# Set attention, then a SoLU layer: product sums of three groups in one PSUM bank, gathers riding with scores, rows scaled by two engines

## The chip, the cores and the metric

The kernel runs on one core of one Trainium2 chip. The metric is the device time of one execution, in microseconds (us); less is better. TensorE is called PE here, VectorE DVE, ScalarE ACT, GpSimd POOL, and SyncE, which issues the transfers, SP.

## The reference

Everything is float32. `x` is 4 x 12608 x 128, there are 32 inducing points, and the layer is 1024 wide.

```python
def mab(q, kv):                       # scale = 1 / sqrt(128)
    s = scale * (q @ kv.transpose(0, 2, 1))
    s = s - s.max(-1, keepdims=True)
    a = np.exp(s)
    a /= a.sum(-1, keepdims=True) + 1e-09
    return a @ kv
h = mab(I, x)                         # 32 inducing points attend to x: first attention
x = mab(x, h)                         # x attends to the 32 rows of h: second attention
h = x @ w_in                          # 128 -> 1024: first layer
e = np.exp(h - h_max)                 # h_max: maximum of the row
solu = h * (e / (e.sum(-1) + 1e-09))
ln = (solu - mean) / np.sqrt(var + 1e-06) * g_ln
out = ln @ w_out                      # 1024 -> 128
```

## The kernel before

Each batch has 12608 rows, which are 99 tiles of 128 (the last is half a tile). The kernel is a set of Python generators, one for each chain of work, and a `Planner` that runs them on a model of the engines before anything is issued: each `Op` names an engine, an assumed cost, what it waits for and a priority, and the planner picks, for the engine that is free first, the ready operation of the lowest priority number (ready within `SLACK` of that engine). The order in which it picks is the order in which the instructions stand on each engine's queue, and each queue runs in that order. Constants named `PR_...`, `SLACK`, `BEAT`, `SWITCH` and so on only steer this order. A `Lock` is a pool of buffers; taking one makes the next instruction wait for the last reader of it.

The work, by generator:

- `p1(b, k)`: first attention on a group of up to 16 tiles (12 in batch 0, which runs first and by itself, "early"). It loads x (`xn`), turns it on PE (L583 in row mode, L614 early), copies it (L593 on ACT), stores the transposed x to DRAM (`xd`, L624), computes the scores (L643), takes the maximum of each column block (L659), brings the four blocks' maxima together with a small product against the matrix `fold` (L663 on DVE, L668 on PE, L677 and L684 on DVE), takes the exp (L694), transposes it on DVE (L714), and sums x with these weights on PE (L725, "the gather"), which DVE adds to a running sum (L741). Groups of the next batch run between the tiles of this one.
- `combine(b)`: finishes h for a batch and folds it into w_in (L772 scales the sum, L790 is the product).
- `p2(b, j)`: second attention's weights for 16 tiles: loads the transposed x back (L818), scores (L833), maximum, subtraction on POOL (L845), exp (L852), turns (L875), copy to `aT` (L889).
- `main()`: for each tile the first layer (L1009), eight products on two of PE's four row blocks, into one of four PSUM buffers `h` of 128 x 1024.
- `soft(...)`: DVE scales the row and finds its extreme (L1050), ACT takes the exp (L1061), POOL multiplies (L1065), ACT squares and sums (L1076), DVE transposes 32 x 32 blocks into `vt` (L1089). A row's buffers come from the pools `HN` and `EU`.
- `products(b, j, t, w)`: four tiles are a group `j`; its second-layer products (L1132) are 4 x 32 of 32 rows against `wc`, with the row sum as a 129th column. The four row blocks `a` go in two pairs `w`, each pair into one `h` buffer. `beats` issues them in beats: in each beat one product of both row blocks of pair 0 and of pair 1, or of one pair while `also`, the first layer or a turn, uses the other pair's row blocks. A beat in which only two of the four row blocks work is called a half beat below.
- `evacuate(...)`: copies a group's pair (2 x 129 columns) from PSUM to `spare`, on DVE or ACT (L1155).
- `floor`: sends the groups' sums of squares through DRAM to their places (`dd`, `dl`).
- `finish(b, f)`: for five groups (`FG`) small ACT and POOL operations make the inverse deviation `y` (L1177 to L1191), then POOL scales each group's rows (L1198), and `stored` writes 256 KB.

PE's scores, gathers and fold products use other modes than the row mode of the rest; the planner adds `SWITCH` for each such visit.

Of the kernel before, what the change touches and what calls it, by code (L numbers as in the profile page):

```python
# [14 lines left out]
ALU = mybir.AluOpType  # L15
# [4 lines left out]
P = 128  # L20
# [14 lines left out]
SWITCH = 400  # L35

# [19 lines left out]
HN_MORE = 4  # L56
# [12 lines left out]
PR_G2 = 8  # L69
PR_HN = -4  # L70
PR_MU = -4
PR_SQ = 4
PR_TU = 12
# [8 lines left out]
WIN = -18.5  # L82
# [8 lines left out]
DMA_LAG = 1800  # L91
# [159 lines left out]
def set_attention_then_solu_kernel(ctx: ExitStack, tc: tile.TileContext, x, inducing, w_in, w_out, g_ln, out):  # L251
# [67 lines left out]
    EW = Lock()  # L319
    ST = Lock([  # L320
# [9 lines left out]
    SM = Lock([small(i, mloc=1, mdiag=4, junk=4, nb=1, fac=1, ls=1, rl=1) for i in range(4)])  # L330
# [200 lines left out]
    turned = [Event() for _ in range(NP[0])]  # L531

    def p1(b, k):
# [35 lines left out]
        def by_rows(ways):  # L569
# [4 lines left out]
            def turn():  # L574
                w = min(ways, key=lambda w: (load(w) > 0, w))
# [9 lines left out]
                beats(-(-n // 2), (1 - w,), two)  # L585

# [47 lines left out]
        if not early:  # L634
            (eT, ew), erel = yield lew
# [11 lines left out]
        d = yield Op("PE", (0 if early else SWITCH) + n * 60, scores, ready, rel, ind_ready.after)  # L647
# [9 lines left out]
        for lo, hi, nn in parts:  # L657
            d = yield Op(
                "DVE", 411, lambda: nc.vector.tensor_reduce(out=v["mloc"][lo:hi], in_=sc[lo:hi, : nn * M], op=ALU.max, axis=AX.X), dsc  # L659
            )  # L660
        d = yield Op(
            "DVE", 131,
            lambda: nc.vector.tensor_scalar(  # L663
                out=v["mdiag"], in0=quarter, scalar1=v["mloc"], scalar2=None, op0=ALU.mult, op1=ALU.max, accum_out=v["nb"]
            ),
            d,
        )
        d = yield Op("PE", (80 if early else SWITCH) + 110, lambda: nc.tensor.matmul(mq, lhsT=fold2, rhs=v["mdiag"], start=True, stop=True), d)  # L668
# [6 lines left out]
        d = yield Op(  # L675
            "DVE", 122,
            lambda: nc.vector.tensor_scalar(  # L677
                out=v["junk"], in0=mq, scalar1=(-3.0e38 if first else mold), scalar2=None, op0=ALU.max, op1=ALU.max, accum_out=mnew
            ),
            d, prev,  # L680
        )
        plan.set(chain[b][k + 1], d)
        dm = d = yield Op(
            "DVE", 70, lambda: nc.vector.tensor_scalar(out=v["nb"], in0=mnew, scalar1=-scale, scalar2=None, op0=ALU.mult), d  # L684
        )
        df = None
        if early:
            (eT, ew), erel = yield lew
# [9 lines left out]
        de = d = yield Op("ACT", (130 + 35 * n) * len(parts) + (0 if first else 190), exps, dm, erel)  # L698
# [15 lines left out]
        d = yield Op("DVE", 435, lambda: nc.vector.transpose(out=ew[:, :n, :].rearrange("p s m -> p (s m)"), in_=eT[:, : n * M]), d)  # L714
        nq = min(4, n)
        rel = None
        if not early:
            give(lpb, big, de)
            big, rel = yield lpb
        pooled = big[:, 512 - C : 512]  # L720

        def gather():
# [6 lines left out]
        dp = yield Op("PE", 74 * n, gather, d, rel)  # L729
# [20 lines left out]
        give(lpb, big, da)  # L750
# [9 lines left out]
    def combine(b):  # L760
# [11 lines left out]
        d = yield Op("DVE", 200, lambda: nc.vector.tensor_scalar(out=accn, in0=acc, scalar1=rl, scalar2=None, op0=ALU.mult), d, prev)  # L772
# [33 lines left out]
    def p2(b, j):  # L806
# [4 lines left out]
        for k, (g0, gn) in enumerate(p1_groups[b]):  # L811
# [47 lines left out]
        def turned_rows():  # L859
# [4 lines left out]
            def turn():  # L864
                w = min(ways, key=lambda w: (load(w) > 0, w))
# [11 lines left out]
                beats(-(-pairs // 2), (1 - w,), two)  # L877

# [40 lines left out]
    stream = [dict(j=JB, emit=None, ready=0.0, close=None) for _ in range(2)]  # L919
    flow = {"idle": Event(), "left": 2 * NB * NG, "prio": 0.0}  # L920

    def load(w):
        p = stream[w]
        return JB - p["j"] if p["j"] < JB and p["ready"] <= plan.now + EAGER else 0

    def beats(count, pairs=(0, 1), also=None):

        for i in range(count):
            if also:
                also(i)  # L930
            went = False
            for w in pairs:
                p = stream[w]
                if p["j"] < JB and p["ready"] <= plan.now + i * BEAT + EAGER:
# [381 lines left out]
```

## Time and profile before

| | us |
|---|---|
| median of 3 runs | 1245.16 (1244.42 to 1248.59) |
| the profiled execution | 1244.09 |
| its span in the profile | 1242.3 |
| busy PE / DVE / ACT / POOL | 1196.1 / 1092.8 / 1085.6 / 1087.8 |
| busy share PE / DVE / ACT / POOL | 96% / 88% / 87% / 88% |
| granted PE clock | 0.979 |
| DMA moved | 113.61 MB, mean 91 GB/s |

Busy time counts every stretch in which at least one instruction of the engine runs. Matmuls overlap each other and their ends are modelled, so PE's share says little about how much of its peak is used. In a view of instruction groups a row reads: line, engine, operation, output and input by the program's names, shape, count, busy time and mean ns of one, and idle time in front of it with what ended it. A wait "A <- B: 28.2, 29, 6.1" means that A's engine stood 28.2 us in all, 29 times and at most 6.1 us, until B was done.

### The profile page before, as it was taken

The page shows a single profiled execution, that of the slowest core. Times are in us where ns is not written, and L with a number is a line of the kernel's source. Part 1 is how long each engine was busy: PE and PEld are TensorE (multiplying, and loading weights), DVE is VectorE, ACT ScalarE, POOL GpSimd, SP SyncE. Part 2 cuts the span into 40 slices and gives each one's busy share as a digit, 9 for nine tenths or more (in the row PEclk, how much of TensorE's full clock was granted, in tenths as well). Part 3 has the DMA queues.
Part 4 walks back from the last instruction along what each step waited for, and adds up shares of the span by engine and source line. Part 5 has one row for each costly group of instructions (what it writes and reads, how often), then busy time and mean ns, then how long its engine had stood idle before and what let it go on. Part 6 is the DMA issues. An engine that isn't in the chain of part 4 may idle for free. (4 is left out here: it accounts for less than half of the span.)

```text
span 1242.3 us, 77962 instructions
## 1 busy us (share of the span) xinstructions
PE 1196.1 (96%) x35557; PEld 1112.9 (90%) x35557; DVE 1092.8 (88%) x1684; ACT 1085.6 (87%) x2152; POOL 1087.8 (88%) x638
## 2 busy tenths in 40 slices
PE   9999999999999989999999999999999999999995
PEld 7679999999998988998999899999899999999995
DVE  5689999999897989899988889989899999898982
ACT  5489998999897979898889889999888999998983
POOL 3478898988987878989898898989898999998996
PEclk9969999999999999999999999999999999989998
DMA  9663243321234233331223333523220212112013
GB/s 355 234 166 111 72 135 90 101 68 38 81 90 130 82 102 110 94 104 50 73 56 108 103 112 101 158 57 110 63 54 16 73 48 61 47 19 48 6 47 85
DMA packets 152908, 113.61 MB, mean 91 GB/s; under 512 B 76257, under 2 KB 132609, under 8 KB 148097
## 3 DMA queue, kind: packets, MB, share of 16 engines
q1 hardware_dynamic: 152576, 108.62, 29.2%
q8 instruction: 278, 4.55, 1.6%
q14 instruction: 54, 0.43, 0.1%
HBM read 54.30 MB, written 52.18 MB: 86 GB/s over the span
## 5 line engine op out<-in xcount | busy, mean ns | idle before, releaser
L1132 PE MATMUL h<-wc,vt 32*128 32x129 f32 (+1 forms) x25600 | 1030.4, 275 | 22.4 <-issue 13.7
L1132 PEld LDWEIGHTS h<-wc,vt 32*128 32x128 f32 (+1 forms) x25600 | 992.7, 186 | 60.6 <-issue 38.6
L1065 POOL TENSOR_TENSOR eu<-spare,eu 128x1024 f32<-128x1024 f32 x227 | 535.7, 2376 | 45.3 <-ACT eu L1061 45.0
L1089 DVE STREAM_TRANSPOSE vt<-eu 128x1024 f32<-128x1024 f32 x396 | 481.6, 1230 | 13.5 <-POOL eu L1065 12.9
L1076 ACT ACTIVATE sq<-eu 128x1024 bf16<-128x1024 f32 x396 | 416.7, 1052 | 47.5 <-POOL eu L1065 37.0
L1009 PE MATMUL h<-hs,aT 32*128 32x128 f32 x6336 | 435.2, 276 | 4.1 <-ACT aT L889 1.7
L1065 POOL TENSOR_TENSOR eu<-hn,eu 128x1024 f32<-128x1024 f32 x169 | 399.7, 2377 | 38.9 <-ACT eu L1061 38.7
L1009 PEld LDWEIGHTS h<-hs,aT 32*128 32x128 f32 x6336 | 392.2, 189 | 23.2 <-issue 6.7
L1050 DVE TENSOR_SCALAR_CACHE_REDUCE spare<-h,rn 128x1024 f32<-128x1024 f32 x227 | 285.8, 1265 | 40.4 <-PE h L1009 23.8
L1061 ACT ACTIVATE eu<-spare,nm 128x1024 f32<-128x1024 f32 x227 | 259.1, 1142 | 10.3 <-DVE spare L1050 7.8
L1050 DVE TENSOR_SCALAR_CACHE_REDUCE hn<-h,rn 128x1024 f32<-128x1024 f32 x169 | 212.8, 1264 | 29.9 <-PE h L1009 17.0
L1061 ACT ACTIVATE eu<-hn,nm 128x1024 f32<-128x1024 f32 x169 | 192.9, 1142 | 7.4 <-DVE hn L1050 4.8
L1198 POOL TENSOR_TENSOR spare<-spare,fin 128x512 f32<-128x512 f32 x100 | 101.2, 1044 | 1.4
L1076 ACT ACTIVATION_READ_ACCUMULATOR sq<-eu 128x1 f32 x396 | 74.8, 189 | 0.0
L1155 ACT COPY spare<-h 128x258 f32<-128x258 f32 (+1 forms) x127 | 45.7, 364 | 29.4 <-PE h L1132 28.2
L583 PE MATMUL h<-ident,xn 32*128 32x32 f32 x1188 | 54.1, 225 | 0.3 <-issue 0.3
L583 PEld LDWEIGHTS h<-ident,xn 32*128 32x128 f32 x1188 | 50.4, 136 | 0.7 <-issue 0.5
L593 ACT COPY xT<-h 128x1024 f32<-128x1024 f32 (+2 forms) x42 | 37.8, 901 | 10.1 <-PE h L583 9.8
L1155 DVE COPY spare<-h 128x258 f32<-128x258 f32 (+1 forms) x73 | 30.2, 416 | 18.4 <-PE h L1132 18.0
L1061 ACT ACTIVATION_READ_ACCUMULATOR eu<-spare,nm 128x1 f32 x227 | 43.0, 190 | 0.0
L875 PE MATMUL h<-ident,a 32*128 32x32 f32 (+1 forms) x800 | 34.2, 221 | 1.4 <-ACT a L852 1.1
L889 ACT COPY aT<-h 128x512 f32<-128x512 f32 (+3 forms) x66 | 30.2, 472 | 5.6 <-PE h L875 5.5
(154 smaller groups left out, 655.2 us busy)
## 6 DMA issues: line engine op xcount, KB each, us to landing
out_dram<-spare SPq DMA_DIRECT2D x96, 256.0 KB, 3.7
xT<-xd SPq DMA_DIRECT2D x19, 1024.0 KB, 5.7
xn<-in_x_dram SPq DMA_DIRECT2D x15, 1024.0 KB, 6.3
xd<-xT SPq DMA_DIRECT2D x15, 1024.0 KB, 5.1
dl<-dd SPq DMA_DIRECT2D x396, 1.0 KB, 2.8
xd<-vt SPq DMA_DIRECT2D x7, 768.0 KB, 10.3
spare<-in_x_dram SPq DMA_DIRECT2D x5, 768.0 KB, 12.8
xT<-xd SPq DMA_DIRECT2D x5, 768.0 KB, 5.6
```

The source lines that it names most:

```text
L583: nc.tensor.transpose(out=tr[:, k * 512 + s * M : k * 512 + (s + 1) * M], in_=xn[r, s, :], identity=ident[r, r])
L593: lambda: nc.scalar.copy(xT.rearrange("c s (q t) -> c q s t", q=4)[:, 2 * w : 2 * w + 2, :n, :], tr.rearrange("c (k x) -> c k x", k=2)[:, ...
L875: nc.tensor.transpose(out=tr[:h, k * 512 + q * M : k * 512 + (q + 1) * M], in_=both, identity=ident[r, r])
L1009: nc.tensor.matmul(hp[:, cols], lhsT=aT[rows, i // 2, :], rhs=hs[rows, cols], start=True, stop=True)
L1050: lambda: nc.vector.tensor_scalar(out=hn, in0=hp, scalar1=rn, scalar2=None, op0=ALU.mult, op1=ALU.min, accum_out=nm),
L1061: "ACT", 1133, lambda: nc.scalar.activation(e, hn, AF.Exp, bias=nm, scale=-1.0, accum_out=G["qe"][:, s, 1:2]), d, rel, srel,
L1065: d = yield Op("POOL", 2330, lambda: nc.gpsimd.tensor_tensor(out=e, in0=hn, in1=e, op=ALU.mult), de, prio=t + PR_MU)
L1076: "ACT", 1040, lambda: nc.scalar.activation(sq, e, AF.Square, scale=1.0 / 32.0, accum_out=G["qe"][:, s, 0:1]), d,
L1089: lambda: nc.vector.transpose(out=G["vtb"][:, : n * FF].rearrange("p (j s t) -> p j s t", j=M, s=n)[:, :, s, :], in_=e.rearrange("p (a f) ...
L1132: nc.tensor.matmul(op[:rows, a - 2 * w, : C + 1], lhsT=vt[q, k, :], rhs=wc[q, k, :], start=(k == 0), stop=(k == JB - 1))
L1155: return lambda: eng(F["raw"][:rows, i0 : i0 + 2, :], op[:rows, :, : C + 1])
L1198: return lambda: eng.tensor_tensor(out=raw, in0=raw, in1=y[:, i0 : i0 + 4].unsqueeze(2).to_broadcast([rows, 4, C]), op=ALU.mult)
```

## The change

- *Products.* Up to three groups in a row (`SLOTS`; 3 and 2 of a finish's five, and 3, 1, 1 in a batch's last) share one `h` buffer per pair, at column offsets of 129. It is taken at the first group and copied once, after the last, by `evacuate` for all of them. `stream[w]` becomes a list, so that the next group's products follow without a gap where they are ready.
- *First attention after batch 0.* The four blocks' maxima are brought together by DVE with one-column reduces (L710 and the like, on 32 partitions) instead of `fold`; ACT scales the maximum. The gather of group k-1 is issued right behind the scores of group k, into the unused half of the same buffer; only a batch's last gather still has a visit of its own.
- *Transfers.* x, the transposed x and its reload go in pieces of four tiles, 256 KB (`PIECE`), at most four under way (`TOKENS`, `BULK`). Batch 0's are left as they were.
- *Scaling.* Scaling the rows has an alternative on ACT, four instructions of 128 columns (`each_quarter`); the planner takes the one that it expects to end first.
- Numbers: priorities, slacks, assumed costs, one `HN` buffer handed to `EU`, three first-layer turns (`MINE`) instead of two, only the nearest tile considered (`WINDOW_TILES`). `accn` is scaled by ACT.

The numbers move almost every row, so the order is shown at three places. On PE, in the first attention of batch 3, which runs between batch 2's tiles, the three visits before: scores (L643), fold (L668) and gather (L725), each between products (L1132) or first layer (L1009); `h_694` and so on are the four buffers.

```order
L1132 MATMUL h_694<-wc,vt 128x129 x4
L643 MATMUL h_697<-xT,indT 32x512 x4
L1009 MATMUL h_696<-hs_117,aT_94 128x128 x2
...
L1132 MATMUL h_695<-wc,vt 128x129 x2
L668 MATMUL h_697<-small_123,fold 128x4
L1132 MATMUL h_694<-wc,vt 128x129 x2
...
L1132 MATMUL h_696<-wc,vt 128x129 x2
L725 MATMUL h_697<-xn_68,ew 32x128 x16
L1009 MATMUL h_695<-hs_117,aT_94 128x128 x2
```

and in the changed program, where L668 is now the scores, L784 the gather, L1244 the products and L1115 the first layer:

```order
L1244 MATMUL h_652<-wc,vt 128x129 x2
L1244 MATMUL h_651<-wc,vt 128x129 x2
L668 MATMUL h_650<-xT,indT 32x512 x4
L784 MATMUL h_650<-xn_68,ew 32x128 x16
L1115 MATMUL h_649<-hs_117,aT_94 128x128 x2
L1244 MATMUL h_652<-wc,vt 128x129 x2
```

The gather of the group before stands directly behind the scores and in their buffer, and the fold row is gone. Over the whole order there are 21 fold rows fewer and 18 gathers without a visit of their own. The products, first layer and turns make 3974 beats with all four row blocks and 536 half beats before, 4063 and 358 after; half beats followed by a full one are 179 and 95.

On ACT, around a finish of five groups, before (L1061 exp, L1076 square, L1155 evacuation, L1177 to L1190 the inverse):

```order
L1076 ACTIVATE sq,qe_100<-eu 128x1024
L1180 ACTIVATE fin_111<-fin_111 128x20
L1155 COPY spare<-h_696 128x258
L1184 ACTIVATE fin_111<-fin_111 128x20
L1185 ACTIVATE fin_111<-fin_111 128x20
L1186 ACTIVATE fin_111<-fin_111 128x20
L1190 ACTIVATE fin_111<-fin_111 128x20
L1061 ACTIVATE eu,qe_102<-hn_82,nm_112 128x1024
```

and after (L1168 exp, L1183 square, L1322 scaling of two groups, L1272 evacuation):

```order
L1168 ACTIVATE eu,qe_106<-hn_81,nm_115 128x1024
L1183 ACTIVATE sq,qe_106<-eu 128x1024
L1322 ACTIVATE spare<-spare,fin_111 128x128 x8
L1168 ACTIVATE eu,qe_100<-hn_80,nm_112 128x1024
...
L1168 ACTIVATE eu,qe_100<-spare,nm_115 128x1024
L1272 COPY spare<-h_652 128x2x2x129
L608 COPY xT<-h_650 128x2x7x32
```

Eight instructions in a row scale two groups; the copy takes two groups at once. Of the 100 scalings 39 stand on ACT, of the evacuations 57 on ACT and 31 on DVE (127 and 73 before).

On SP, around a reload of the transposed x, before (L818 reload, L624 store, L364 load of x, L1106 and L1114 the sums of squares):

```order
L1106 DMA dd_105<-qe_104 128x8
L818 DMA xT_86<-xd 128x2048
L1114 DMA dl_110<-dd_105 32x4x2 x4
L1106 DMA dd_107<-qe_106 128x8
L1114 DMA dl_110<-dd_107 32x4x2 x4
L364 DMA xn_67<-in_x_dram 128x4x512
```

and after (L899, L642, L371, L1213, L1221):

```order
L642 DMA xd<-xT 128x512 x4
L1213 DMA dd_103<-qe_102 128x8
L1221 DMA dl_108<-dd_103 32x4x2 x4
L371 DMA xn_68<-in_x_dram 128x512 x3
L899 DMA xT_86<-xd 128x512
L1213 DMA dd_105<-qe_104 128x8
L371 DMA xn_68<-in_x_dram 128x512
L899 DMA xT_86<-xd 128x512 x2
```

Pieces of two transfers now alternate with each other and with the small ones; SP issues 912 transfers instead of 736.

The diff, cut to its core:

```diff
+OS_ACT = 1
+SLOTS = 3
+PIECE = 4
+TOKENS = 4
-HN_MORE = 4
+HN_MORE = 3
-PR_G2 = 8
+PR_G2 = 4
...
-SLACK = {"PE": 0, "ACT": 200, "DVE": 100, "POOL": 100, "SP": 0}
+SLACK = {"PE": 0, "ACT": 400, "DVE": 200, "POOL": 100, "SP": 0}
-WINDOW_TILES = 3
-MINE = 2
-OP_FIRST = -30
+WINDOW_TILES = 1
+MINE = 3
+OP_FIRST = -100
...
+        if not early:
+            halves = [(c, min(c + PIECE, n)) for c in range(0, n, PIECE)]
         for c0, c1 in halves:
             for nbytes, fn in move(b, s0 + c0, c1 - c0, xn[:, c0:, :], False):
-                d = yield dma(nbytes, fn, rel)
+                trel = () if early else (yield BULK)[1]
+                d = yield dma(nbytes, fn, rel, trel)
+                if not early:
+                    give(BULK, None, d)
...
+        def visit():
+            scores()
+            if before:
+                gathers[(b, k - 1)](big[:, 512 + P : 512 + P + C])
...
+            def near():
+                for g in range(1, 4):
+                    same(v["quart"][quad[0], g : g + 1], v["quart"][quad[g], 0:1])
...
+            def spread():
+                for g in range(1, 4):
+                    same(mnew[quad[g]], mnew[quad[0]])
...
     def products(b, j, t, w):
-        bank, rel = yield H.at(OP_FIRST + t)
-        op = bank.rearrange("p (k x) -> p k x", k=2)
+        slot, last = slot_of[j]
+        if slot == 0:
+            held[w] = yield H.at(OP_FIRST + t)
+            held[w] += ([],)
+        bank, rel, mine = held[w]
+        mine.append(j)
+        op = bank.rearrange("p (k x) -> p k x", k=2)[:, :, slot * (C + 1) : (slot + 1) * (C + 1)]
...
         def close(d):
-            spawn(evacuate(b, j, w, op, bank, d, t + PR_EV), t + PR_EV)
+            if last:
+                spawn(evacuate(b, mine, w, bank, d, t + PR_EV), t + PR_EV)
+                give(PAIR[w], None)
...
-        stream[w].update(j=0, emit=emit, ready=ready, close=close, prio=t + PR_G2)
+        stream[w].append(dict(j=0, emit=emit, ready=ready, close=close, prio=t + PR_G2))
...
+            def each_quarter():
+                for a in range(4):
+                    act(raw[:, a, :], raw[:, a, :], AF.Copy, scale=y[:, i0 + a : i0 + a + 1])
+
-            done = yield Op("POOL", 1000, scaled(nc.gpsimd), dy, prio=OS_PRIO)
+            done = yield Op("POOL", 1000, scaled(nc.gpsimd), dy, prio=OS_PRIO, alt=Op("ACT", 1010, each_quarter, dy, prio=OS_PRIO) if OS_ACT else None)
```

More of the change, by code (lines that the diff above doesn't have):

```diff
@@ L633, in p1 @@
             yield ind_ready
-        if not early:
-            (eT, ew), erel = yield lew
+        before = None
+        if not early and k:
+            before = yield weighed[(b, k - 1)]
         big, rel = yield lpb
@@ L645, in scores @@
                 )
-        d = yield Op("PE", (0 if early else SWITCH) + n * 60, scores, ready, rel, ind_ready.after)
+        def visit():
+            scores()
+            if before:
+                gathers[(b, k - 1)](big[:, 512 + P : 512 + P + C])
+        d = yield Op(
+            "PE", (SWITCH + 74 * (p1_groups[b][k - 1][1] if before else 0) if not early else 0) + n * 60, visit, ready, rel, ind_ready.after, before
+        )
+        if before:
+            pooled_in[(b, k - 1)] = big[:, 512 + P : 512 + P + C]
+            plan.set(gathered[(b, k - 1)], d)
         def free_xT():
@@ L727, in gather @@
                 )
-        dp = yield Op("PE", 74 * n, gather, d, rel)
+        if not early:
+            if k:
+                give(lpb, big, de, *p1_added[(b, k - 1)].after)
+            else:
+                give(lpb, big, de)
+        if early or k == NP[b] - 1:
+            rel = None
+            if not early:
+                big, rel = yield lpb
+            pooled = big[:, 512 - C : 512]
+            dp = yield Op("PE", (0 if early else SWITCH) + 74 * n, lambda: gather(pooled), d, rel)
+            own = True
+        else:
+            gathers[(b, k)] = gather
+            plan.set(weighed[(b, k)], d)
+            got = yield gathered[(b, k)]
+            dp, pooled, own = got[0], pooled_in[(b, k)], False
         give(lx, xn, dp)
@@ L749, in p1 @@
         da = yield Op("DVE", 263, add, dp, de, p1_done[b][k - 1].after if k else None)
-        give(lpb, big, da)
+        if own:
+            give(lpb, big, da)
+        plan.set(p1_added[(b, k)], da)
         dl = yield l_done[b][k]
@@ L771, in combine @@
         prev = yield p1_done[b][NP[b] - 1]
-        d = yield Op("DVE", 200, lambda: nc.vector.tensor_scalar(out=accn, in0=acc, scalar1=rl, scalar2=None, op0=ALU.mult), d, prev)
+        d = yield Op("ACT", 200, lambda: nc.scalar.activation(accn, acc, AF.Copy, scale=rl), d, prev)
         give(SM, v, d)
@@ L917, in set_attention_then_solu_kernel, with going @@
     grp = {(b, j): dict(vt=Event(), st=Event(), floor=Event(), turned=[], squared=[], over=[]) for b in range(NB) for j in range(NG)}
-    stream = [dict(j=JB, emit=None, ready=0.0, close=None) for _ in range(2)]
-    flow = {"idle": Event(), "left": 2 * NB * NG, "prio": 0.0}
+    slot_of, held = {}, [None, None]
+    for f in range(-(-NG // FG)):
+        js = [j for j in range(NG) if j // FG == f]
+        while js:
+            same = [j for j in js[:SLOTS] if ff_groups[j][1] == ff_groups[js[0]][1]]
+            for i, j in enumerate(same):
+                slot_of[j] = (i, j == same[-1])
+            js = js[len(same) :]
+    stream = [[], []]
+    flow = {"idle": Event(), "left": 2 * NB * NG, "half": False, "took": 0}
+    def going(w, at):
+        for p in stream[w]:
+            if p["j"] < JB:
+                return p if p["ready"] <= at + EAGER else None
+        return None
     def load(w):
-        p = stream[w]
-        return JB - p["j"] if p["j"] < JB and p["ready"] <= plan.now + EAGER else 0
+        return going(w, plan.now) is not None
     def beats(count, pairs=(0, 1), also=None):
+        flow["took"] = 0
         for i in range(count):
```

193 lines of the change are left out of this document (120 added, 73 removed).

## The prediction

> **What bounds the kernel now.** I read the busy table cut into stages first, then the sums of waits, then the chain that ended last, and single rows of the timeline for prices. The stages are cut where the score rows of a batch's 99 tiles have passed: 58 us ends the first attention of batch 0, and 350, 645, 935 and 1212 us end the four batches.
>
> ```profile
> core 0: us, PE busy (x) PEld busy (x) DVE busy (x) ACT busy (x) POOL busy (x), PEclk, DMA share, GB/s
> 58.00:350.00 292.00, 287.91 (x8454) 264.34 (x8454) 269.55 (x415) 264.93 (x516) 257.17 (x138) 0.96 0.33 95
> 350.00:645.00 295.00, 284.00 (x8650) 262.58 (x8646) 260.92 (x398) 260.59 (x514) 257.85 (x150) 0.99 0.31 93
> 645.00:935.00 290.00, 283.77 (x8778) 264.36 (x8773) 268.05 (x416) 264.21 (x517) 264.04 (x154) 1.00 0.32 94
> 935.00:1212.00 277.00, 271.34 (x8549) 264.87 (x8544) 253.15 (x339) 256.18 (x510) 269.65 (x152) 0.98 0.17 40
> 1212.00:1243.00 31.00, 16.29 (x576) 15.91 (x570) 6.14 (x7) 9.94 (x27) 19.46 (x22) 0.81 0.32 85
> ```
>
> In the three stages that still prepare a next batch PE is busy 96 to 99% and the other engines 87 to 92%. In the last, which prepares none, POOL is the fullest of the others at 269.65 of 277 us, 97.3%. PE's busy time is modelled and overlaps itself, so its 98% there proves little; the chain decides.
>
> ```profile
> 737.35 1.98 PE h L1132 x55
> 740.52 2.58 PE h L1132 x89
> ...
> 1043.84 16.39 POOL eu L1065 x8
> ...
> 1136.98 34.23 POOL eu L1065 x15
> ...
> 1184.34 5.04 POOL spare L1198 x5
> ...
> 1214.06 14.58 PE h L1132 x512
> ```
>
> The chain runs over PE's products (L1132) up to about 935 us and over POOL afterwards, and there L1198, which scales the output rows, stands in it with 1.01 us for each of five. The tail is the last products, whose 512 records (eight to a full beat, 64 beats) give the price of a beat: 14.58 / 64 = 0.228 us.
>
> ```profile
> POOL eu L1065 <- ACT eu L1061: 83.7, 54, 6.3
> ACT sq L1076 <- POOL eu L1065: 37.0, 43, 2.8
> ACT spare L1155 <- PE h L1132: 28.2, 29, 6.1
> DVE spare L1050 <- PE h L1009: 23.8, 30, 5.1
> DVE spare L1155 <- PE h L1132: 18.0, 21, 6.6
> DVE hn L1050 <- PE h L1009: 17.0, 19, 2.4
> ```
>
> In the waits, ACT and DVE stand 28.2 and 18.0 us in front of evacuations (L1155) whose products are not done, with exps and transposes queued behind, and DVE 23.8 + 17.0 = 40.8 us for the first layer (L1009). These are waits for a late PE. POOL's 83.7 us for the exp is the same lateness passed on.
>
> **The change, part by part.** *Visits of PE outside its row mode.* Fold matrix (L668) and gather (L725) in the timeline:
>
> ```profile
> 787.15 1.83 PE L1132 MATMUL h<-wc,vt 32*128 32x129 f32 x47
> 789.08 1.08 PE L725 MATMUL h<-xn,ew 128*32 128x128 f32 x32
> 790.09 0.38 PE L1009 MATMUL h<-hs,aT 32*128 32x128 f32 x2
> ...
> 807.35 2.06 PE L1132 MATMUL h<-wc,vt 32*128 32x129 f32 x66
> 809.34 0.39 PE L668 MATMUL h<-small,fold 128*128 128x4 f32 x2
> 809.66 0.60 PE L1132 MATMUL h<-wc,vt 32*128 32x129 f32 x6
> ...
> 1013.67 0.72 PE L1009 MATMUL h<-hs,aT 32*128 32x128 f32 x10
> ```
>
> The last product before the fold starts at 807.35 + 2.06 - 0.28 = 809.13 and the next at 809.66; undisturbed it would have been 0.11 later, so a fold costs 0.42 us. All 21 of the later batches go: 8.8 us. Eighteen of the 21 gathers move behind the next group's scores, which use the same column mode. Around 789.08 the way in costs 0.27 us (788.70 to 789.08 less 0.11) and the way out 0.21 (from the gather's last start, 789.88). I take 0.4 for each visit spared, 7.2 us; the bounds are nothing and 0.48. By stage, 13, 14, 12 and 0 visits disappear.
>
> *Beats.* A bank now takes three groups in turn, so the next group's products are ready to fill a beat when one group ends, instead of waiting for a copy and a bank. Counted over PE's order, 3974 full and 536 half beats become 4063 and 358. A half beat is no shorter (the ten records at 1013.67 start over 0.44 us, four per 0.22). So 89 beats of 0.228 are 20.3 us less: 19, 19, 4, 40 beats in the four stages and 7 in the tail. The beats' own first-after-a-switch cost is within nothing and 0.1 us for some 84 fewer half-to-full changes; I add 4 us. PE in all: -40 us, or by stage -10, -11, -7, -10, and -2 in the tail.
>
> *Scaling by two engines.* Of the 100 L1198 rows, 39 become four ACT instructions each (5, 10, 10, 10 in the stages, 4 in the tail).
>
> ```profile
> L1198 POOL TENSOR_TENSOR spare<-spare,fin 128x512 f32<-128x512 f32 x100 | 101.2, 1044 | 1.4
> L460 ACT ACTIVATE hn<-hn,g_sb 128x128 f32<-128x128 f32 x8 | 2.9, 393 | 0.0
> L561 ACT COPY vt<-bank_e 128x512 f32<-128x512 f32 x23 | 12.1, 593 | 10.8 <-PE bank_e L614 10.8
> L593 ACT COPY xT<-h 128x1024 f32<-128x1024 f32 x30 | 30.0, 1000 | 9.4 <-PE h L583 9.1 <-PE h L1132 0.2
> L1155 DVE COPY spare<-h 128x258 f32<-128x258 f32 x72 | 29.8, 416 | 11.8 <-PE h L1132 11.4
> L840 DVE STREAM_TRANSPOSE s<-h 128x512 f32<-128x512 f32 x19 | 13.2, 696 | 2.4 <-PE h L833 2.3
> L772 DVE TENSOR_SCALAR accn<-acc,small 128x128 f32<-128x128 f32 x4 | 3.7, 930 | 0.0
> L659 DVE TENSOR_REDUCE small<-h 128x1 f32<-128x512 f32 x15 | 10.3, 687 | 1.1 <-PE h L643 1.1
> L659 DVE TENSOR_REDUCE small<-h 64x1 f32<-64x192 f32 x3 | 1.1, 360 | 0.1
> L663 DVE TENSOR_SCALAR_CACHE_REDUCE small<-quarter,small 128x4 f32<-128x4 f32 x30 | 6.0, 199 | 0.4
> ```
>
> ```profile
> 49.85 0.70 ACT L460 ACTIVATE hn<-hn,g_sb 128x128 f32<-128x128 f32 x2
> ...
> 1061.12 0.35 ACT L1155 COPY spare<-h 128x258 f32<-128x258 f32 x1
> 1061.37 1.15 ACT L1061 ACTIVATE eu<-spare,nm 128x1024 f32<-128x1024 f32 x1
> ```
>
> POOL loses 39 x 1.01 = 39 us. L460 is the same form (128 columns, a scale per row): 0.39 us alone, but two in 0.70, so a following one adds 0.31, and a set of four costs about 1.2 us: ACT +47 us (bounds 39 x 4 x 0.25 = 39 and 39 x 4 x 0.39 = 61). Sets come in pairs, up to 2.4 us in which no exp starts; POOL has three of its own to do then.
>
> *Evacuations.* ACT's 127 become 26 of three groups, 21 of two, 10 of one. A small copy occupies ACT 0.25 us (1061.12 to 1061.37), 0.1 less than its row. From the 593 and 1000 ns rows, 774 columns take 0.80 and 516 take 0.60, so 0.70 and 0.50 occupied: 18 + 10.5 + 2.5 = 31 against 32 us, no change. DVE's 73 become 14, 11 and 6, from the 416 and 696 ns rows 14 x 0.98 + 11 x 0.70 + 6 x 0.42 = 24 against 30 us: -6. The gain is in the waits: 88 stops instead of 200.
>
> *Maxima without the fold.* On DVE, per group, two reducing operations like L663 and a small one go (about 0.7 us) and six reduces of one column, one reducing operation come. The two L659 rows fall 1.02 ns a column, which leaves 0.165 us at one: 6 x 0.165 + 0.28 = 1.27, +0.57 x 21 = +12 us; at least 0.1 each (no change), at most 0.36 each (+37). The L772 rows (3.7 us) leave DVE. DVE in all: +2 us, so nothing. ACT gets 21 small scalings and the four L772: +4 us.
>
> *x in pieces.*
>
> ```profile
> out_dram<-spare SPq DMA_DIRECT2D x96, 256.0 KB, 3.7
> xT<-xd SPq DMA_DIRECT2D x19, 1024.0 KB, 5.7
> ```
>
> SP issues 912 transfers instead of 736, four bulk pieces at most under way; a fifth holds SP until the first lands, and the row sums (dd, dl) and output rows queue behind it. Four in flight land little later than one of 1 MB (bounds: 5.7 us, and one after another 4 x 3.7 = 14.8). I cost it at nothing: second attention's loads start 35 tiles ahead, 35 x 2.95 = 103 us. If that cover went, 9 us a load would show. [...]
>
> *Priorities, slacks and buffers* (one product buffer fewer for hn, one more for eu, three tiles ahead instead of two) only move instructions; their effect is in the beat counts and the rest is rival matter.
>
> **The sum.** ACT's demand becomes 265 + 6 + 1 = 272, 261 + 12 + 1 = 274, 264 + 12 + 1 = 277, 256 + 12 = 268. It is the fullest engine beside PE. I let it fill a stage as far as POOL fills the last one now, 97.3%: 279.5, 281.6, 284.7 and 275.4. PE asks for 292 - 10 = 282, 295 - 11 = 284, 290 - 7 = 283, and in the last stage for less. Taking the later of the two and one us for each where both are near: 283, 285, 285, 276, which is -9, -10, -5, -1. POOL falls to 259.5 in the last stage, so ACT takes its place there. The tail loses 7 beats (1.6) and about one of its L1198: -2.5. Sum -27.5 from the profiled execution's 1244.1 us (span 1242.3, 1.8 around it; 1.1 under the median of 1245.2): 1216.6. With the median, 1217; I say 1216.
>
> **The rivals.**
> - *PSUM starves the first layer* (slower). The two product streams now hold a bank each over three groups, nine tenths of the time, where 32 beats of a group's 11.9 us held it some six tenths. Two of four are left for the first layer, transposes, scores and sums. If DVE's 40.8 us of waits for L1009 doubled, 1216 + 41 = 1257; from 28 us of new waits (0.07 per tile) the gain is gone. For it: the longest of those waits is 5.1 us already. Against: the sum of visits goes down and three tiles may be ahead. [...]
> - *ACT saturates sooner.* It has reached 92.5% at most in a stage. At 95%: (272 + 274 + 277 + 268) / 0.95 = 1148 for 1154, 1244 - 6 - 2.5 = 1235. For it: strict turns, pairs of sets in front of exps. Against: 28 us of its present waits are for evacuations.
> - *Everything interlocks better.* Fewer stops let ACT fill 98.5% and PE lose its waits: 276, 279, 281, 272, which is -46 and -2.5: 1195.
> - *PE was not the limit*, and its savings come back as waits while POOL's and ACT's exchange evens out: 1244.
> - *Pieces block SP.* If four loads came late by the 9 us: 1216 + 36 = 1252.
>
> **Chances.** The forecast 0.46 (its own range 1203 to 1228), PSUM 0.13, ACT 0.17, interlocking 0.17, no effect 0.04, pieces 0.03. This kernel's measurement cannot tell 0.3% (1241 to 1249) from no change. Faster: 0.46 + 0.17 and most of ACT's 0.17 (0.14) make 0.77; the same: 0.04 and the rest of ACT's, 0.03; slower: PSUM and the pieces, 0.16. From 1190 to 1250 lie all but the worse half of the PSUM case, the pieces, and the best of the interlocking, about 0.8.
>
> **What would show it.** Right: stages of 283 to 285 us in the first three, ACT at 96% or more and fuller than DVE and POOL, 88 evacuations with under 25 us of waits together, no fold rows on PE after 60 us, POOL's wait for the exp under 60 us. Wrong: DVE's waits for the first layer above 60 us (PSUM), or ACT idle before its scaling rows while POOL still works on the inverse, or SP waiting for x while PE idles.

## The result and the profile after

The changed kernel takes 1209.99 us (median of 4, 1207.19 to 1212.33) where the kernel before takes 1246.88 (median of 4 on the same chip): ratio 0.9712 with a 95% interval of 0.9682 to 0.9742, by the ratio 36 us less. The profiled execution took 1207.19 us, its span is 1205.3.

For a comparison by stage I cut both traces at one kind of event: POOL's multiply of a batch's first tile (L1065 before, L1172 after), and the end of the last multiply. These cuts lie 1 to 20 us from those of the prediction (954.90 for its 935, 1219.60 for its 1212), so its forecasts, in the last column of the table below, are for slightly other stretches. The busy table before:

```profile
core 0: us, PE busy (x) PEld busy (x) DVE busy (x) ACT busy (x) POOL busy (x), PEclk, DMA share, GB/s
57.20:353.70 296.50, 292.26 (x8550) 268.45 (x8551) 274.01 (x421) 269.43 (x524) 259.47 (x140) 0.97 0.33 97
353.70:656.60 302.90, 292.05 (x8935) 270.60 (x8933) 268.83 (x410) 268.45 (x530) 266.27 (x151) 0.99 0.31 91
656.60:954.90 298.30, 291.86 (x9037) 271.51 (x9037) 273.91 (x423) 270.57 (x533) 270.35 (x161) 1.00 0.30 88
954.90:1219.60 264.70, 258.96 (x8161) 253.49 (x8158) 239.74 (x319) 243.96 (x480) 261.01 (x145) 0.97 0.18 42
1219.60:1242.50 22.90, 8.98 (x324) 8.76 (x319) 2.09 (x3) 4.23 (x16) 11.86 (x19) 0.75 0.41 113
```

and after:

```profile
53.60:350.20 296.60, 288.53 (x8514) 265.09 (x8512) 275.98 (x430) 277.29 (x541) 255.13 (x136) 0.95 0.35 98
350.20:639.50 289.30, 282.57 (x8954) 264.02 (x8956) 273.27 (x424) 277.83 (x559) 257.78 (x142) 1.00 0.33 94
639.50:922.20 282.70, 277.02 (x8862) 258.68 (x8858) 269.38 (x416) 274.37 (x557) 257.69 (x144) 1.00 0.33 93
922.20:1182.50 260.30, 254.10 (x8284) 246.18 (x8284) 244.19 (x318) 253.50 (x512) 254.42 (x140) 0.99 0.18 43
1182.50:1205.50 23.00, 9.45 (x332) 9.00 (x324) 2.09 (x3) 9.21 (x32) 7.85 (x14) 0.80 0.41 113
```

| stretch | before | after | change | forecast |
|---|---|---|---|---|
| head | 57.2 | 53.6 | -3.6 | none |
| batch 0 | 296.5 | 296.6 | +0.1 | -9 |
| batch 1 | 302.9 | 289.3 | -13.6 | -10 |
| batch 2 | 298.3 | 282.7 | -15.6 | -5 |
| batch 3 | 264.7 | 260.3 | -4.4 | -1 |
| rest (to the span's end) | 22.7 | 22.8 | +0.1 | -2.5 |

The gain lies in batches 1 and 2. In the rows of batches 1 to 3 ACT, beside PE, is now the fullest or level with POOL: 277.83 of 289.30 is 96.0%, then 97.1% and 97.4%. The sums of waits after:

```profile
POOL eu L1172 <- ACT eu L1168: 69.2, 78, 3.2
POOL spare L1172 <- ACT spare L1168: 20.2, 16, 3.4
DVE spare L1157 <- PE h L1115: 12.4, 16, 2.4
DVE spare L1272 <- PE h L1244: 10.1, 6, 6.9
ACT spare L1272 <- PE h L1244: 9.5, 11, 3.1
DVE hn L1157 <- PE h L1115: 7.9, 12, 1.3
```

The waits for a late PE have halved: 19.6 us in front of evacuations (L1272) where there were 46.2, 20.3 for the first layer (L1115) where there were 40.8. POOL waits as much for the exp as before (89.4 us in two rows, 83.7 before), so that wait was not only PE's lateness passed on, as the prediction read it. The groups that the change made:

```profile
L1322 ACT ACTIVATE spare<-spare,fin 128x128 f32<-128x128 f32 x156 | 47.9, 390 | 0.8 <-POOL fin L1311 0.7
L1272 ACT COPY spare<-h 128x774 f32<-128x774 f32 (+3 forms) x57 | 36.6, 644 | 13.2 <-PE h L1244 9.5
L1318 POOL TENSOR_TENSOR spare<-spare,fin 128x512 f32<-128x512 f32 x61 | 61.8, 1040 | 1.5
L710 DVE TENSOR_REDUCE m<-m 32x1 f32<-32x1 f32 x63 | 9.1, 145 | 1.3
L710 DVE TENSOR_REDUCE small<-small 32x1 f32<-32x1 f32 x63 | 9.0, 143 | 1.3
```

ACT scales 39 groups in 156 instructions for 47.9 us; POOL keeps 61. The chain that ended last, by engine, before and after:

```profile
POOL 16%; PE 16%; ACT 4%; issue 2%; DVE 2%; POOLq 0%; DMA 0%; ACTq 0%; DVEq 0%
```

```profile
PE 11%; ACT 3%; DVE 2%; issue 1%; POOL 0%; DMA 0%; SPq 0%; POOLq 0%; ACTq 0%; DVEq 0%
```

These chains reach back only to 737 us before and to 991 us after, so they cover 40% and 17% of the span, the last batch above all. (The prediction speaks of PE's products "up to about 935 us": the view shows this from 737 us on only.) POOL's 16%, nearly all of them from 955 us on, are gone. What took their place is PE, 11 of the 17%, and not ACT, to which the prediction gave it and which has 3%. The issues of x and the instruction queue, in the transfers' view:

```profile
q8 instruction: 277, 4.54, 1.6%
...
xT<-xd SPq DMA_DIRECT2D x96, 256.0 KB, 4.1
...
xn<-in_x_dram SPq DMA_DIRECT2D x73, 256.0 KB, 4.0
xd<-xT SPq DMA_DIRECT2D x72, 256.0 KB, 2.8
```

A piece lands in 2.8 to 4.1 us. A row `q8 instruction` stands before and after alike (278 packets before); it comes to matter below.

### The profile page after: what moved, and what is told of

Its sections match the earlier page's. It is cut to its first block, busy times and chain, and to the rows that moved or that the text cites. A ratio compares the mean times of both kernels' runs of the same rounds, so it can differ in the third digit from the quotient of the medians.

```text
span 1205.3 us, 78134 instructions
## 1 busy us (share of the span) xinstructions
PE 1159.9 (96%) x35487; PEld 1079.9 (90%) x35487; DVE 1098.2 (91%) x1701; ACT 1119.5 (93%) x2263; POOL 1050.5 (87%) x599
## 3 DMA queue, kind: packets, MB, share of 16 engines
q1 hardware_dynamic: 171392, 108.63, 31.2%
q8 instruction: 277, 4.54, 1.6%
## 5 line engine op out<-in xcount | busy, mean ns | idle before, releaser
L1244 PE MATMUL h<-wc,vt 32*128 32x129 f32 (+1 forms) x25600 | 996.2, 274 | 15.5 <-issue 6.2
L1244 PEld LDWEIGHTS h<-wc,vt 32*128 32x128 f32 (+1 forms) x25600 | 961.3, 185 | 46.9 <-issue 27.3
L1172 POOL TENSOR_TENSOR eu<-hn,eu 128x1024 f32<-128x1024 f32 x197 | 464.1, 2374 | 34.6 <-ACT eu L1168 33.9
L1115 PE MATMUL h<-hs,aT 32*128 32x128 f32 x6336 | 438.4, 278 | 7.2 <-DVE spare L1157 1.7
L1115 PEld LDWEIGHTS h<-hs,aT 32*128 32x128 f32 x6336 | 393.2, 190 | 26.2 <-issue 6.7
L1196 DVE STREAM_TRANSPOSE vt<-eu 128x1024 f32<-128x1024 f32 x330 | 402.2, 1230 | 7.6 <-POOL eu L1172 7.5
L1183 ACT ACTIVATE sq<-eu 128x1024 bf16<-128x1024 f32 x330 | 346.1, 1049 | 6.2 <-POOL eu L1172 1.9
L1172 POOL TENSOR_TENSOR eu<-spare,eu 128x1024 f32<-128x1024 f32 x133 | 314.1, 2373 | 35.3 <-ACT eu L1168 35.3
L1168 ACT ACTIVATE eu<-hn,nm 128x1024 f32<-128x1024 f32 x197 | 224.4, 1139 | 1.6 <-DVE hn L1157 1.0
L1172 POOL TENSOR_TENSOR spare<-spare 128x1024 f32<-128x1024 f32 x65 | 154.5, 2376 | 20.3 <-ACT spare L1168 19.4
L1168 ACT ACTIVATE eu<-spare,nm 128x1024 f32<-128x1024 f32 x133 | 151.5, 1139 | 0.6 <-DVE spare L1157 0.3
L1196 DVE STREAM_TRANSPOSE vt<-spare 128x1024 f32<-128x1024 f32 x66 | 81.0, 1228 | 0.0
L1168 ACT ACTIVATE spare<-spare,nm 128x1024 f32<-128x1024 f32 x65 | 74.0, 1138 | 0.3 <-DVE spare L1157 0.3
L1183 ACT ACTIVATE sq<-spare 128x1024 bf16<-128x1024 f32 x66 | 69.2, 1049 | 1.2 <-ACT sq L1183 0.4
L1183 ACT ACTIVATION_READ_ACCUMULATOR sq<-eu 128x1 f32 x330 | 62.6, 190 | 0.0
L1272 ACT COPY spare<-h 128x774 f32<-128x774 f32 (+3 forms) x57 | 36.6, 644 | 13.2 <-PE h L1244 9.5
L1322 ACT ACTIVATE spare<-spare,fin 128x128 f32<-128x128 f32 x156 | 47.9, 390 | 0.8 <-POOL fin L1311 0.7
```

What stands on the lines that cost most here:

```text
L1115: nc.tensor.matmul(hp[:, cols], lhsT=aT[rows, i // 2, :], rhs=hs[rows, cols], start=True, stop=True)
L1168: "ACT", 1133, lambda: nc.scalar.activation(e, hn, AF.Exp, bias=nm, scale=-1.0, accum_out=G["qe"][:, s, 1:2]), d, rel, srel,
L1172: d = yield Op("POOL", 2330, lambda: nc.gpsimd.tensor_tensor(out=e, in0=hn, in1=e, op=ALU.mult), de, prio=t + PR_MU)
L1183: "ACT", 1040, lambda: nc.scalar.activation(sq, e, AF.Square, scale=1.0 / 32.0, accum_out=G["qe"][:, s, 0:1]), d,
L1196: lambda: nc.vector.transpose(out=G["vtb"][:, : n * FF].rearrange("p (j s t) -> p j s t", j=M, s=n)[:, :, s, :], in_=e.rearrange("p (a f) ...
L1244: nc.tensor.matmul(op[:rows, a - 2 * w, :], lhsT=vt[q, k, :], rhs=wc[q, k, :], start=(k == 0), stop=(k == JB - 1))
```

## The experiments

Ratios are to the kernel before, timed on the same chip in the same batch of runs. Differences to the changed kernel are the difference of the ratios (its own is 0.9712) times 1245 us. E1 to E4 ran on a chip on which the kernel before took 1250.24 us, so a time there reads some 3 us high against an expectation that reckons from the result. E1 to E4 undo one part each, E5 to E8 ask how sizes and numbers share the gain, E9 and E10 isolate the transfers, E11 tests the bound, E12 goes further in the direction that won.

### E1: all scaling on POOL

```diff
-OS_ACT = 1
+OS_ACT = 0
```

> The changed kernel, but all 100 row scalings stay on POOL (POOL +39 us, ACT -47). The re-planned order has 64 beats more (3999 full, 486 half). Theory 1, PE's order and its stops carry the gain and the exchange of POOL for ACT is nearly even: 64 x 0.228 = 15 us of beats, some of it beside other work, 2 us more in the tail, the last stage shorter since ACT is relieved: 1214 to 1224 us. Theory 2, the relief of POOL carries the gain: 1235 us or more, POOL over 97% in every stage.

Measured: 1225.43 us, 0.9817 [0.9760, 0.9873], 13 us more than the changed kernel. POOL's busy time goes from 1050.5 back to 1087.6 us, ACT's from 1119.5 to 1082.6. The sharing is worth 13 us here, as the first theory had it, but all of that may come by way of the order: without the sharing the planner makes 64 beats more (3999 full and 486 half, where there were 4063 and 358), which at 0.228 us are 14.6 us.

### E2: one group in a bank

```diff
-SLOTS = 3
+SLOTS = 1
```

> The changed kernel, but each group's products take a bank of their own and are copied by themselves (200 evacuations instead of 88; 3966 full and 552 half beats, 97 beats more). Theory 1: 97 x 0.228 = 22 us and the stops in front of evacuations come back (46 us of waits instead of 20): 1230 to 1242 us. Theory 2: PE is not what ends the stages, 1210 to 1218 us. If a bank held over three groups starves the first layer, DVE's waits for it (20 us in the changed kernel) fall.

Measured: 1229.0 us, 0.9841 [0.9784, 0.9898], 16 us more. Beats are 3966 full and 552 half. Waits of this kernel:

```profile
ACT spare L1272 <- PE h L1244: 22.6, 31, 4.4
DVE spare L1272 <- PE h L1244: 19.6, 15, 6.7
...
DVE spare L1157 <- PE h L1115: 10.5, 17, 1.3
...
DVE hn L1157 <- PE h L1115: 8.6, 15, 1.0
```

The waits for evacuations are back at 42.2 us, those for the first layer do not fall (19.1 for 20.3): a bank held over three groups does not starve the first layer. The 16 us lie between the two theories: 97 beats more were to cost 97 x 0.228 = 22 us of PE, and the stops in front of evacuations came on top, so a beat is worth less at the end than its time on PE.

### E3: the gather by itself

```diff
         before = None
-        if not early and k:
-            before = yield weighed[(b, k - 1)]
...
-        if early or k == NP[b] - 1:
+        if True:
```

> The changed kernel, but each later gather is a visit of its own again (18 visits more, beats as they were, 4063 and 358). Theory 1: 18 x 0.4 = 7 us: 1216 to 1219 us. If ACT, not PE, ends the stages now: 1210 to 1213 us.

Measured: 1217.69 us, 0.9747 [0.9703, 0.9792], some 4 us more, with an interval that overlaps the changed kernel's. The beats stay at 4063 and 358, so this is the 18 visits alone: 0.2 us each by the medians, half of the 0.4 that I gave them. The two intervals together leave some 7 us either way, so neither nothing nor the whole 0.4 is ruled out.

### E4: the maxima by the fold again

```diff
-        if early:
+        if True:
...
             d = yield Op(
...
+            d = yield Op("PE", (80 if early else SWITCH) + 110, lambda: nc.tensor.matmul(mq, lhsT=fold2, rhs=v["mdiag"], start=True, stop=True), d, added)
```

> The changed kernel, but the four blocks' maxima are brought together by the fold product on PE again (21 visits more, 4 beats fewer, DVE about 10 us and ACT 3 us less). Theory 1: 21 x 0.42 - 1 = 8 us: 1215 to 1219 us. If ACT and DVE end the stages now, the two sides cancel: 1207 to 1212 us.

Measured: 1215.53 us, 0.9714 [0.9652, 0.9777]: no difference that shows, with some 9 us left open either way. By the ratio this is the second theory's case; the time alone, on that chip, would pass for the first's. PE has its 21 fold visits again, but DVE gets back the time of the one-column reduces (busy 1082.4 us for 1098.2).

### E5: pieces as large as the whole moves

```diff
-PIECE = 4
-TOKENS = 4
+PIECE = 16
+TOKENS = 64
```

> The changed kernel with x, the transposed x and its reload moved in whole groups again (736 transfers) and no limit on those under way. Its re-planned order has 45 beats more (4018 full, 448 half). Theory 1: the cut into pieces is hidden either way, what shows is the plan: up to 45 x 0.228 = 10 us, 1210 to 1220 us against 1250 of before on this chip (ratio 0.968 to 0.980). Rival: pieces kept the small transfers and PE's turns on time, so without them 1225 us or more (ratio over 0.98) and longer waits of SP.

Measured: 1241.22 us, 0.9947 [0.9914, 0.9980]. The loss is 29 us, most of the gain. Theory 1 missed; the ratio is in the rival's range, and SP does wait longer (156.9 us for `dd`, where the changed kernel has 127.9). But the planner also made another order (4018 full and 448 half beats), so order and transfers are mixed. The profiled execution, whose rows follow, is the slowest of ten, at 1249.61 us. What stood out was PE, waiting for nothing that the profile shows ("issue"), 48.8 us on the weight loads and 24.5 on the products:

```profile
PEld h L1244 <- issue: 48.8, 61, 3.2
PE h L1244 <- issue: 24.5, 25, 3.0
```

### E6 and E7: structure and numbers apart

E6 has the new structure with the constants of before (slacks, priorities, `MINE`, `WINDOW_TILES` and the like), E7 the structure of before with the new constants:

```diff
-SLACK = {"PE": 0, "ACT": 400, "DVE": 200, "POOL": 100, "SP": 0}
+SLACK = {"PE": 0, "ACT": 200, "DVE": 100, "POOL": 100, "SP": 0}
...
-WINDOW_TILES = 1
-MINE = 3
+WINDOW_TILES = 3
+MINE = 2
```

> The changed kernel's structure with the old numbers (priorities, slacks, buffers, look-ahead). Beats 4039 full, 406 half (24 more than the changed kernel), 46 scalings on ACT. Theory 1, structure carries the gain: two thirds of it or more stay, ratio to before 0.970 to 0.982. Rival, the numbers carry it: ratio over 0.985.

> The kernel before with the new numbers alone. Beats 3905 full, 674 half (69 more than before, 16 us). Theory 1: no gain, rather slower, ratio 1.000 to 1.014. Rival, the numbers carry the gain: ratio under 0.985.

Measured: E6 1237.52 us, 0.9925 [0.9898, 0.9951], where 0.970 to 0.982 was expected, and over 0.985 if the numbers carry the gain; E7 1258.93 us, 1.0102 [1.0051, 1.0152], as expected. The structure alone gains 9 us, the numbers alone lose 13, both together gain 36. So neither theory holds: each needs the other. Why E6 falls so far short was not found; its 24 beats more are 5.5 us by their price. In E6 POOL waits 113.8 us for the exp:

```profile
POOL eu L1172 <- ACT eu L1168: 113.8, 85, 5.4
```

### E8: one group of each five on ACT

```diff
-... dy, prio=OS_PRIO) if OS_ACT else None)
+... dy, prio=OS_PRIO) if j == js[1] else None)
```

> The changed kernel, but only one of a finish's five groups may be scaled on ACT (18 sets instead of 39: ACT -25 us, POOL +21 us; beats 4032 full, 420 half, 31 more). If ACT's load ends the stages: 1200 to 1208 us (ratio 0.960 to 0.968). Theory 1 with the plan's beats: 1211 to 1217 us (ratio 0.970 to 0.977).

Measured: 1218.83 us, 0.9770 [0.9724, 0.9816]. With 0, 18 and 39 groups on ACT (E1, E8, the changed kernel) the ratio is 0.9817, 0.9770, 0.9712: in a line, 0.33 us for each group that leaves POOL, though neighbours' intervals overlap. The ratio is at the upper end of theory 1. ACT is busy 1097.6 us here, 22 less than in the changed kernel, and the time is longer all the same, so the first case of the expectation, that ACT's load ends the stages, did not come. The beats lie in the same line, 64 and 31 more than in the changed kernel, 14.6 and 7.1 us at 0.228 for 13 and 7 measured. So these two runs cannot tell the relief of POOL from the order that comes with it; at 39 the two together still pay.

### E9: the same order, moves whole

Here nothing is planned anew: the order on PE, ACT, DVE and POOL is that of the changed kernel, row for row. Where its first piece of a move stands on SP, the whole 1 MB move is issued, and the other pieces are left out.

```diff
                 lambda: nc.sync.dma_start(
-                    xT[:, c0:c1, :].rearrange("p s t -> p (s t)"), xT_dram[b][:, (s0 + c0) * P : (s0 + c1) * P]
-                ),
+                    xT[:, :n, :].rearrange("p s t -> p (s t)"), xT_dram[b][:, s0 * P : (s0 + n) * P]
+                ) if c0 == 0 else None,
```

This is the reload's place; the loads of x and the stores of the transposed x are changed in the same way.

> The changed kernel with the order of PE, DVE, ACT and POOL kept row for row; only on SP the first piece of each move carries the whole group (1 MB) and the other pieces are left out. Theory 3, a large transfer delays the fetching of PE's instructions, seen as stalls of PE with nothing waited for some 4 to 7 us after it is issued: those stalls rise from 8 us to 20 us or more, 1220 to 1232 us (ratio 0.976 to 0.986). Rival, e5 lost by its plan's 45 beats alone: 1207 to 1214 us (ratio 0.967 to 0.974), stalls as in the changed kernel.

Measured: 1231.03 us, 0.9845 [0.9790, 0.9901], 17 us more than the pieces. The waits have the same form as in E5:

```profile
PEld h L1248 <- issue: 51.0, 56, 3.1
PE h L1248 <- issue: 27.6, 25, 2.9
```

In the changed kernel these two rows are 27.3 and 6.2 us. By the same cuts as above, the stages of batches 2 and 3 in this kernel:

```profile
647.40:946.30 298.90, 282.27 (x8859) 262.61 (x8858) 269.88 (x416) 275.35 (x557) 257.77 (x145) 0.98 0.30 88
946.30:1207.50 261.20, 255.10 (x8280) 247.40 (x8276) 244.33 (x319) 253.40 (x512) 254.29 (x140) 0.99 0.18 43
```

ACT, DVE and POOL are busy for as long as after the change, to 1 us; the stages are 299.1, 294.9, 298.9 and 261.2 us, that is +2.5, +5.6, +16.2 and, where the DMA share is 0.18, +0.9. Pauses of PE over 1 us (counted as below) grow by 8.3, 7.8, 13.2 and 0.4 us in these stages, so batch 0 hides most of its own. The longest of PE's pauses, in PE's timeline:

```profile
724.87 1.39 PE L1248 MATMUL h<-wc,vt 32*128 32x129 f32 x40
729.21 2.21 PE L1248 MATMUL h<-wc,vt 32*128 32x129 f32 x45 [2.94 <-issue]
```

SP's queue just ahead of it:

```profile
719.27 1.15 SPq L903 DMA_DIRECT2D xT<-xd  x1
...
721.11 0.62 SPq L646 DMA_DIRECT2D xd<-xT  x1
```

and the DMA view of the window from 726.2 to 729.3 us, packets, MB and share of the 16 engines:

```profile
q1 hardware_dynamic: 733, 1.16, 98.9%
q8 instruction: 1, 0.02, 1.9%
```

Two moves of 1 MB and some output rows are under way, the engines are 98.9% busy, and one packet of the instruction queue passes. It starts at 726.78 us, 0.8 us after PE's last start, takes 0.95 us, which is usual (mean 1.08 over all), and PE starts again 1.47 us after it landed. That it is an instruction packet of PE fits the counts: 277 packets of 16 KB are 4.54 MB, which over PE's 70,974 instructions (products and weight loads) is 64 bytes for one and 256 instructions in a packet, an estimate that takes all of them as PE's. So I read the pause as PE out of instructions because a packet came late. The place of the pauses and E10, below, test this.

I then counted in the traces all pauses of PE over 1 us after 60 us (between starts), and of these the ones that end 1.1 to 1.8 us after such a packet landed. With a packet each 4.3 us a pause falls there by chance one time in six.

| kernel | pauses | of these behind a packet |
|---|---|---|
| before | 13, 22.7 us | 8, 15.2 us |
| after | 7, 9.6 us | 3, 4.1 us |
| E5, whole moves | 21, 38.3 us | 15, 29.4 us |
| E9, whole moves, same order | 23, 39.3 us | 19, 34.2 us |
| E10, idle copies, same order | 16, 25.2 us | 11, 18.8 us |
| E12, half pieces | 9, 15.1 us | 3, 3.7 us |

The place fits too: four of E9's pauses in a row (at 729, 744, 769 and 781 us) stand at PE's instructions 40855, 41623, 43158 and 43670, which are 768, 1535 and 512 apart, multiples of 256 within one. Of all 19, 18 keep this step: divided by 256, their places leave a remainder that falls steadily from 173 at the first (187 us) to 142 at the last (975 us). The nineteenth, at 33882, is a pause of the changed kernel too. E5's row of the table is, like its rows above, of the slowest execution.

### E10: copies that nobody waits for

The pieces stay; behind each reload of a whole group a copy of 1 MB from DRAM to DRAM is issued whose result nothing reads (29 of them). The order is again that of the changed kernel.

```diff
+        def beside(c1):
+            if c1 == n:
+                nc.sync.dma_start(idle_copy, xf[: AG * P, :])
...
+                    beside(c1),
```

> The changed kernel, its order kept, plus 29 copies of 1 MB from DRAM to DRAM behind the reloads of the transposed x, whose result nothing uses. Theory 3: PE's stalls with nothing waited for rise from 8 us to 15 us or more, 1215 to 1228 us (ratio 0.972 to 0.983). Rival, a large transfer hurts only who waits for its data: 1207 to 1214 us.

Measured: 1230.34 us, 0.9858 [0.9813, 0.9902], 18 us more, a little over the range of theory 3. PE's waits, and the copies:

```profile
PEld h L1253 <- issue: 37.3, 51, 2.2
...
PE h L1253 <- issue: 14.8, 16, 2.2
```

```profile
idle_copy<-in_x_dram SPq DMA_DIRECT2D x29, 7.2
```

This meets the main objection: in E9 the data themselves land at other times, here they only have company. Copies of which no instruction needs anything made PE pause (third column of the table, 4.1 to 18.8 us). Real pieces behind them on SP may be late as well, so not all of the 18 us need be PE's instructions.

### E11: the scaling done twice on ACT

Each of the 156 scalings is followed by a second one into a scratch tile, which nothing reads; the order of all else is unchanged.

```diff
                     act(raw[:, a, :], raw[:, a, :], AF.Copy, scale=y[:, i0 + a : i0 + a + 1])
+                    act(sq[: raw.shape[0], :C], raw[:, a, :], AF.Copy, scale=y[:, i0 + a : i0 + a + 1])
```

> The changed kernel, its order kept, with each of the 156 scaling instructions on ACT followed by an equal one into a scratch tile (ACT +48 us). If ACT ends the stages of the changed kernel: 30 to 48 us more, 1240 to 1258 us (ratio 0.992 to 1.006). If PE ends three stages of four: up to 20 us more, under 1231 us (ratio under 0.985).

Measured: 1279.9 us, 1.0249 [1.0209, 1.0288], 67 us more. The two groups, original and added:

```profile
L1323 ACT ACTIVATE sq<-spare,fin 128x128 bf16<-128x128 f32 x156 | 62.7, 402 | 5.1
...
L1322 ACT ACTIVATE spare<-spare,fin 128x128 f32<-128x128 f32 x156 | 60.5, 388 | 0.8 <-POOL fin L1311 0.7
```

ACT is busy 1182.7 us, 63 more and not the 48 that the changed kernel's row suggests. In a row of four, each scaling starts 0.29 us after the one before and overlaps it. Here the added one starts 0.42 us after its original, just behind its end, and the next original 0.31 us after the added one, so a pair takes 0.73 us. All 63 us come out at the end, and 4 more. In the order as planned ACT has no slack, and the rival in this expectation, under 20 us more since PE ends three stages, is wrong. But work added on ACT also holds up PE (its products' wait for ACT's evacuations, L1272, goes from 4.8 to 12.6 us), and E9 and E10 cost 17 and 18 us with ACT's busy time as it was (1120.5 and 1120.6 us). So this does not show that ACT alone ends the stages: neither engine has room. (The planner did not know of the added work, so this is the price without any rearrangement.)

### E12: pieces of two tiles

```diff
-PIECE = 4
+PIECE = 2
```

> The changed kernel with pieces of two tiles (128 KB, 1159 transfers) and four under way in the plan. Its re-planned order has 4070 full and 344 half beats (7 fewer). Theory 3: PE's stalls fall under 8 us, 1202 to 1209 us (ratio 0.962 to 0.969). Rival, the issue of 247 more transfers on SP delays the small ones: 1210 to 1220 us.

Measured: 1207.86 us, 0.9674 [0.9636, 0.9713], 5 us less than the changed kernel with overlapping intervals: the best version, but not clearly a better one. Its order is planned anew, with 7 beats fewer. A reload's piece lands sooner, and the longest wait for nothing in front of the products' weight loads falls from 1.4 to 0.8 us:

```profile
xT<-xd SPq DMA_DIRECT2D x196, 128.0 KB, 2.7
```

```profile
PEld h L1244 <- issue: 21.2, 38, 0.8
```

## Why the prediction was right, and where it was not

The time, 1210 for a forecast of 1216, came within the likeliest case's own range, but the medians say that two terms of the sum were wrong in ways that cancel, and the stages came out otherwise, so that the number is so close is in part luck.

- *Beats: right in kind, rather too dear.* The 20 us for 89 beats fewer compare with 16 us in E2, which gives back 97 and the stops too. The 4 us more for 84 fewer changes from half to full beats were not tried alone; in the trace of before PE's first step behind such a change is 0.22 us at 238.58 us and 0.11 at 785.37, where the steps after it are 0.11, so a change costs nothing to 0.11 us there. The stops fell as said: evacuations wait 19.6 us (under 25 was forecast).
- *Visits: too much by 12 us, by the medians.* I gave 8.8 us to the folds and 7.2 to the gathers. E4 shows nothing for the folds, with 9 us open either way, E3 about 4 us for the gathers, with 7. The step that likely failed is to count a visit's PE time as path time: DVE's longer way to the maximum, which I costed at "nothing" beside PE, stands in the same chain of one group (the runs show the net of both, nothing, and not each).
- *Scaling by two engines: sizes right.* 39 sets as in the order, 0.39 us for an instruction, 47.9 us on ACT (47 forecast); POOL lost 37.3 us (39 forecast). ACT's busy time rose by only 33.9 us (51 forecast); in part this is the evacuations' rows, which I had at no change (45.7 us before, 36.6 after; rows overlap others, so not all of it counts). E1 and E8 put the exchange at 13 us, together with the order that comes with it.
- *Pieces at nothing: the failed step.* I looked only at who waits for the data. The whole moves delayed PE without anyone waiting for them, and E9 puts the pieces at 17 us, some 8 either way. The rows that say so stood in the waits before, and I passed them over:

```profile
PEld h L1132 <- issue: 38.6, 53, 2.8
...
PE h L1132 <- issue: 13.7, 12, 2.7
```

- *"A fifth holds SP until the first lands"* was wrong: the four under way are a matter of the plan, not of a wait on SP. The rival that rested on it, blocked pieces, could not come so. The bound of 14.8 us for four pieces one after another did not show either: a piece lands in a median of 2.8 to 4.1 us.
- *Stages.* Batches 1 to 3 with the rest gained 33.5 us where 18.5 was forecast, batch 0 nothing where 9 was. Batch 3 and the rest together became 4.3 us shorter for a forecast of 3.5, the right size, though none of it in the rest: there the second finish begins 9 to 10 us after the last multiply in both, whatever POOL has left: before it stands behind ACT's last copy of the products (at 1228.66 us), after it waits for its row sums to land (`dl<-dd`). That batch 0's stage stays at 296.6 us, with a granted clock of 0.95, and that the head became 3.6 us shorter, no run explains.
- *ACT fills the stages: half right.* I let ACT fill 97.3% of every stage; it reaches 93.5, 96.0, 97.1 and 97.4%. E11 shows that ACT has no slack in the order as planned. It does not end the stages alone: with 37 and 22 us less of it E1 and E8 were slower, E9 and E10 cost time without more work on ACT, and the chain of the last stage runs mostly over PE.
- *The rivals.* PSUM starving did not come (20.3 us of waits for the first layer, where a doubling to 81.6 was the case; E2 shows no relief with banks held for a shorter time). ACT saturating sooner did not come. Interlocking came in part: batches 1 and 2 gained 13.6 and 15.6 us where it gave 16 and 9. POOL's wait for the exp stayed at 89 us, above the 60 that I had named as a sign of being right.

The parts do not add: undone one at a time they cost 13 + 16 + 4 + 0 + 17 = 50 us, together 36 are gained, and structure without its numbers gains 9 (E6), numbers without the structure lose 13 (E7). What each is worth holds only with the others in place. Why the new order with whole moves pauses more than the kernel before (19 and 8 pauses behind a packet) was not tried.

## What to carry to other kernels

Read the waits of an engine for nothing: here PE paused beside transfers of 1 MB, by up to 3.2 us between starts with the moves whole (E9), and also beside copies that nobody waits for (E10, 25.2 us of pauses), and pieces of 256 KB helped (39.3 us of pauses in E9 against 9.6 in the same order). That its instructions, one packet each 4.3 us over the same DMA engines, came late is my reading of the places and counts above. Before an engine's saved time goes into the sum, look at what replaces it on the chain; here a saving that handed the work to an engine nearly as full was worth a third (13 of 37 us) or nothing that shows (the folds). Adding work to one engine does not say that it alone sets the time: here added work on ACT and pauses of PE both came out at the end. Judge structure and planner numbers together, since each alone may lose.

## What the runs showed of the hardware

- In the changed kernel the instruction queue moved 277 packets of 16 KB (4.54 MB), one each 4.3 us, and took 1.6% of the 16 DMA engines' span, the data 31.2%. PE's 70,974 instructions are 256 for a packet, so I read these as PE's instructions. In E9 PE resumes 1.2 to 1.6 us after a packet has landed, in the 18 pauses that keep the step of 256.
- Transfers of 1 MB were the worse choice in this kernel: 17 us slower than 256 KB in the same order (E9, some 8 us either way), while 128 KB was at least as good (E12, 1207.86 us, 5 us less with overlapping intervals).
- Scalings of 128 columns in a row on ACT start 0.29 us apart, each taking 0.39 (the changed kernel). When every second one writes another tile, in bf16, a pair takes 0.73 us: the added one starts 0.42 us after the original, the next original 0.31 us after it (E11). Whether the tile or the type does it was not tried.
